# Moving one constant's load ahead of a weight tile, and a step's weight products ahead of its last attention blocks

## The chip, the cores and the metric

The kernel runs on one core of a Trainium2 chip. Time is device time in microseconds (us). The kernel before has a median of 446.83 us over 6 runs (446.69 to 450.45). The core's engines work side by side, each on its own list of instructions in order: TensorE (PE, with its weight loads PEld), VectorE (DVE), ScalarE (ACT), GpSimd (POOL) and SyncE (SP). Here POOL mostly issues transfers.

## The reference, cut to what matters

Two operators follow each other. The first is causal attention with a forget gate, for 8 batches, 8 heads, 576 positions and head size 64:

```python
scores = scale * q @ k.T                       # (8, 8, 576, 576)
decay  = cum[:, :, :, None] - cum[:, :, None, :]    # cum = cumsum(log(f))
attn   = softmax(where(causal, -1e9, scores + decay))
x      = (attn @ v), heads side by side        # (8, 576, 512)
```

The second mixes x along the sequence in the frequency domain, with one complex 512 x 512 matrix for each of 64 kept modes, and then mixes channels:

```python
X  = rfft(x, axis=1)[:, :64]
Yr = einsum("bmd,mde->bme", Xr, w_r) - einsum("bmd,mde->bme", Xi, w_i)
Yi = einsum("bmd,mde->bme", Xr, w_i) + einsum("bmd,mde->bme", Xi, w_r)
u  = x + irfft(Y, n=576)
out = u + relu(u @ w_ch)
```

`w_r` and `w_i` are 64 x 512 x 512 float32 each, 134 MB together. `w_ch` is 512 x 512 float32. Every weight of `w_r` and `w_i` is used once for each batch.

## The kernel before, in words

**Weights.** The two mode arrays are cut into 64 tiles of two transfers (`w_r`, `w_i`). Each transfer reads 1 MB of float32 and writes 512 KB of bf16, converted on the way. A tile is `emit_w_load(n)` (line 91), issued by POOL at line 89. The tiles live in a ring `wb` of 9 buffers (`NRING`, line 57), so the load of tile n may start only when the products with tile n - 9 are finished. The products are `emit_modes(n)` (line 118): 32 small matmuls into one PSUM tile `A` (line 146; the pool `psM` has one buffer during the attention), then one DVE instruction that stores `A` or adds it into `Yacc` (lines 155 and 157). Tiles 0 to 31 use the channels 0 to 255 of x (`dc` 0 and 1), and tiles 32 to 63 the channels 256 to 511, so that these need the whole attention to be over.

**Attention.** There are 32 steps s: a pair of heads `dc`, a pair of batches `bp`, one head h of the two; two successive steps make a pair `pr`. The loop is at line 649. A step emits, in this order: (a) in an even step the loads of k, q and v for pair `pr + 2` (`emit_loads`, line 215, on POOL); (b) in steps 0 to 8 a further weight tile, up to tile 8, which fills the ring; (c) the transposes of the next pair (`tp`, line 453: k and q in an even step, v in an odd one); (d) the first piece of the step's scores (`ps`, line 505) with their exponential on ACT (`E`, line 512) and the mask on DVE (line 527); (e) the first three row blocks of the product of the previous step's weights with v (`emit_av(s - 1, [0, 1, 2])`: `pav`, line 550, 16 matmuls, then a reciprocal and a scaling on DVE, lines 561 and 572); (f) the second and third piece of the scores; (g) the last two row blocks, `emit_av(s - 1, [3, 4])`, 18 matmuls and two DVE instructions; (h) the fourth, small piece of the scores and `emit_vback(s)` (`vp` and `va`, lines 477 to 484); (i) in an even step the Fourier transform of the pair that is done (`emit_dft`: `px`, lines 593 and 618, into `XT`, line 629). From step 9 on, (j), a step ends with one or two calls of `emit_modes`, each followed by `next_w()` (line 640), the load of the next tile.

**After the attention** (line 756), the tiles 32 to 62 alternate with `emit_xw`, the product of x with `wch` (lines 718 and 729). The last tile and the outputs follow from line 901.

**Order.** POOL's transfers stay in program order (`pool_dma`, line 88), so one that waits holds back all behind it. On the other engines a planner at build time lists the instructions: what is emitted first comes first, but where an instruction isn't ready in the planner's model of the time, a later one that is ready goes ahead of it. So PE's order isn't the order of emission. Before the first k transposes of step 14 (119.55 us) the trace shows 13 blocks of 32 `A` matmuls on PE, while the loop has called `emit_modes` 6 times by the end of step 13. `XT` of `dc` 0, which all of the tiles 0 to 15 need, is complete after the transform that step 8 emits.

`wch` is loaded once, in step 10 (line 656): behind tile 9, which `next_w()` issues at the end of step 9, and behind the k, q and v of pair 7. Its first use is at line 729, at 278.83 us.

Of the kernel before, what the change touches and what calls it, by code (L numbers as in the profile page):

```python
# [15 lines left out]
def _strided(ap: bass.AP, free_dims, offset_elems: int = 0) -> bass.AP:  # L16
    new_ap = [list(ap.ap[0])] + [list(x) for x in free_dims]
    return bass.AP(tensor=ap.tensor, offset=ap.offset + offset_elems, ap=new_ap)
# [3 lines left out]
def kernel(  # L22
# [12 lines left out]
    B, H, S, Dh = q.shape  # L35
# [43 lines left out]
    NTH = NT // 2  # L79
# [3 lines left out]
    def tile_of(n):  # L83
        if n < NTH:
            return divmod(n, NG)
        return 2, (n - NTH + GL) % NTH

    def pool_dma(dst, src):
        tc.keep_in_program_order(nc.gpsimd.dma_start(dst, src))  # L89

    def emit_w_load(n):
        dc, g = tile_of(n)
        if n < NTH:
            wb = wpool.tile([128, MG, 2 * D], BF16, tag="wb", name="wb")
            for t, src in enumerate((moe_w_r, moe_w_i)):
                pool_dma(
                    wb[t:128:2, :, :],
                    src[
                        g * MG : (g + 1) * MG, dc * 128 : (dc + 1) * 128, :
                    ].rearrange("m (p r) e -> p m (r e)", r=2),  # L100
                )
        else:
            wb = wpool.tile([128, 2, M2, 2 * D], BF16, tag="wb", name="wb")
            parts = 2 if n == NT - 1 else 1
            for h in range(parts):
                ms = slice(h * M2 // parts, (h + 1) * M2 // parts)
                for t, src in enumerate((moe_w_r, moe_w_i)):
                    pool_dma(
                        wb[:, t, ms, :],
                        src[g * M2 : (g + 1) * M2, D // 2 : D, :][ms].rearrange(  # L110
                            "m (p r) e -> p m (r e)", r=2
                        ),
                    )
        wtiles[n] = wb
# [3 lines left out]
    def emit_modes(n):  # L118
        dc, g = tile_of(n)
        wb = wtiles.pop(n)  # L120
        nm = MG if n < NTH else M2
        if late["psM"] is None:
            z = late["psZ"].tile([128, 2, D], F32, tag="z", name="A")
            A = z[:, 0, 0 : NDC * nm * 2 * B].rearrange(
                "p (e m c) -> p e m c", e=NDC, m=nm
            )
        else:
            A = late["psM"].tile([128, NDC, nm, 2 * B], F32, tag="A", name="A")
        if n < NTH:
            terms = [  # L130
                (lambda mi, es, r=r: wb[:, mi, r * D + es : r * D + es + 128],
                 lambda m, r=r: XT3s[dc][:, r, :, m])
                for r in (0, 1)
            ]
        else:
            terms = [
                (lambda mi, es, t=t, r=r: wb[:, t, mi, r * D + es : r * D + es + 128],
                 lambda m, c0=c0, r=r: XT3s[2 + r][:, m, c0 : c0 + 2 * B])
                for t, c0 in ((0, B), (1, 0))
                for r in (0, 1)  # L140
            ]
        for mi in range(nm):
            m = g * nm + mi
            for eb in range(NDC):
                for i, (w_of, x_of) in enumerate(terms):
                    nc.tensor.matmul(  # L146
                        A[:, eb, mi, :],
                        lhsT=w_of(mi, eb * 128),
                        rhs=x_of(m),
                        start=(i == 0),  # L150
                        stop=(i == len(terms) - 1),
                    )
        ysl = Yacc[:, :, g * nm : (g + 1) * nm, :]
        if n < NG:
            nc.vector.tensor_copy(ysl, A[:, :, :, :])
        elif n < NTH:
            nc.vector.tensor_tensor(ysl, A[:, :, :, :], ysl, ALU.add)
        else:
            n8 = nm * 2
            yt, w = (late["YTl"], GL * n8) if g < GL else (late["YT"], 2 * NM)  # L160
            nc.vector.tensor_tensor(  # L161
                _strided(
                    yt[:, 0, 0, g * n8 : g * n8 + 1], [[B * w, NDC], [w, B], [1, n8]]
                ),
                _strided(A[:, 0, 0, 0:1], [[nm * 2 * B, NDC], [1, B], [B, n8]]),
                _strided(
                    Yacc[:, 0, g * nm, 0:1], [[NM * 2 * B, NDC], [1, B], [B, n8]]
                ),
                ALU.add,
            )  # L170

    with ExitStack() as actx:
# [42 lines left out]
        def emit_loads(pr):  # L215
            dc, bp, _ = steps[2 * pr]
            for nm, src in (("k", k), ("q", q), ("v", v)):
                one = src[2 * bp, 2 * dc, :, :]
                dst = QKVst[pr % STG][nm][:, :, :, :].rearrange("p b r d -> p b (r d)")
                ap = bass.AP(  # L220
                    tensor=one.tensor,
                    offset=one.offset,
                    ap=[[NR * Dh, 128], [H * S * Dh, 2], [1, NR * Dh]],
                )
                if nm == "v" and pr < 2:
                    nc.sync.dma_start(dst, ap)
                else:
                    pool_dma(dst, ap)
# [268 lines left out]
        def emit_scores(s, piece):  # L497
            E = Es[s % NE]
            w = sum(x[2] for x in PIECES[piece])
            ps = psS.tile([128, 2, 512], F32, tag="sc", name="ps")  # L500
            h, pr = s % 2, s // 2
            for jb, c0, n, o in PIECES[piece]:
                for b in range(2):
                    bs = slice(b * 64, b * 64 + 64)
                    nc.tensor.matmul(  # L505
                        ps[:, b, o : o + n],
                        lhsT=KTs[pr % 2][bs, h, jb * 128 : (jb + 1) * 128],
                        rhs=QT[pr][bs, h, jb * 128 + c0 : jb * 128 + c0 + n],
                        start=True,
                        stop=True,  # L510
                    )
            nc.scalar.activation(  # L512
                E[:, :, piece * 512 : piece * 512 + w],
                ps[:, :, 0:w],
                ACT.Exp,
                scale=scale,
            )
            tri = trimask[:, :]
            if piece == 2:
                dg = _strided(E[:, 0, EOFF[2] : EOFF[2] + 1], [[EW, 2], [320, 2], [1, 128]])  # L520
                tr = _strided(tri, [[0, 2], [0, 2], [1, 128]])
            else:
                jb = {0: 0, 1: 1, 3: 4}[piece]
                n = 64 if piece == 3 else 128
                dg = E[:, :, EOFF[jb] : EOFF[jb] + n]
                tr = _strided(tri, [[0, 2], [1, n]])
            nc.vector.tensor_tensor(dg, dg, tr, ALU.mult)  # L527
# [108 lines left out]
        NS = len(steps)  # L636
        nload = 2
        nmode = 0

        def next_w():  # L640
            nonlocal nload
            if nload < NDC * NG:
                emit_w_load(nload)
                nload += 1
# [4 lines left out]
        for s in range(NS + 1):  # L649
            pr, h = s // 2, s % 2  # L650
            if h == 0 and pr + STG - 1 < NPR:
                emit_loads(pr + STG - 1)
            if s < 10 and nload < min(NRING, 3 + 3 * s // 4):
                next_w()
            if s == 10:
                pool_dma(wch[:], moe_w_ch.rearrange("(eb p) e -> p eb e", p=128))
            if pr + 1 < NPR:
                emit_transposes(pr + 1, ("kq", "v")[h])
            if s < NS:
                emit_scores(s, 0)  # L660
            if s >= 1:
                emit_av(s - 1, [0, 1, 2])
            if s < NS:
                emit_scores(s, 1)
                emit_scores(s, 2)
            if s >= 1:
                emit_av(s - 1, [3, 4])
            if s < NS:
                emit_scores(s, 3)
                emit_vback(s)  # L670
            if s >= 1:
                vaugs.pop(s - 1)
                if h == 0:
                    emit_dft(pr - 1)
            if s > B:
                while nmode < (s - B) * NTH // (NS - B):
                    emit_modes(nmode)
                    nmode += 1
                    next_w()

    with ExitStack() as bctx:
        bsb = bctx.enter_context(tc.tile_pool(name="bsb", bufs=1))
# [255 lines left out]
```

The softmax here doesn't subtract the row's maximum and nothing guards it: scores larger than these inputs give would overflow.

## Time and profile before

| what | value |
|---|---|
| median of 6 runs | 446.83 us |
| profiled execution, its own time | 446.75 us |
| its span, first to last instruction | 445.0 us |
| PE busy | 337.1 us (76%), mean granted clock 0.796 |
| DVE busy | 240.5 us (54%) |
| ACT busy | 197.8 us (44%) |
| POOL's transfers (queue 0) | 85.34 MB, 98.3% of 16 engines over the span |
| read from HBM / written to it | 163.73 MB / 9.44 MB |

Busy times are sums of the instructions' durations. A share of the 16 transfer engines is the time that all packets took over 16 times the stretch, and packets overlap, so a full queue shows 1.1 to 1.2 and not 1.0. GB/s count the bytes written. "Landing" is the time from the issue of a transfer by POOL until its last part has arrived. `[17.32 <-PE A L146]` after an instruction says that its engine stood idle for 17.32 us before it, and what ended the wait.

### The profile page before, as it was taken

The numbers are of one execution on the slowest core, as the hardware profiler recorded it, in microseconds if no ns is written. First come the engines' busy times: TensorE is split into PE (matmuls) and PEld (weight loads), VectorE is DVE, ScalarE is ACT, GpSimd is POOL, SyncE is SP. The second block draws the span as 40 slices with busy tenths as digits, with TensorE's granted clock in tenths as the row PEclk, the third lists the DMA queues.
The fourth block names the chain that finished last, engine by engine and source line by source line (L and its number), as shares of the span: only waits on it lengthen the run. The fifth ranks groups of instructions, "written<-read, shape, count | busy, mean of one in ns | idle before, by whom it ended". The sixth has DMA issues, their size and how long they took to land.

```text
span 445.0 us, 11215 instructions
## 1 busy us (share of the span) xinstructions
PE 337.1 (76%) x4823; PEld 232.7 (52%) x4823; DVE 240.5 (54%) x614; ACT 197.8 (44%) x296; POOL 138.4 (31%) x194
## 2 busy tenths in 40 slices
PE   2388888999797887977878896999982247527993
PEld 1256556687665566656655675566662124323441
DVE  5768988878466564655566675233230002103993
ACT  3378877776344636336536381334420002102442
POOL 7333330532332323323323221132343232200661
PEclk9999999999665857558668596899995558856998
DMA  8999999699999999999999999999999999991697
GB/s 203 211 235 238 237 237 236 116 236 212 236 237 210 237 217 230 237 217 230 237 217 231 211 212 211 211 209 211 211 212 210 211 211 211 211 195 31 224 378 278
DMA packets 50048, 97.27 MB, mean 219 GB/s; under 512 B 3376, under 2 KB 12080, under 8 KB 50000
## 3 DMA queue, kind: packets, MB, share of 16 engines
q0 software_dynamic: 46096, 85.34, 98.3%
q1 hardware_dynamic: 3824, 11.09, 6.9%
q8 instruction: 38, 0.62, 0.5%
q10 hardware_dynamic: 80, 0.13, 0.1%
q14 instruction: 10, 0.08, 0.0%
HBM read 163.73 MB, written 9.44 MB: 389 GB/s over the span
## 4 chain that ended last, share of the span: by engine, by line
PE 45%; DMA 20%; ACT 14%; DVE 10%; issue 4%; POOL 0%; DVEq 0%; ACTq 0%
DMA wb<-in_moe_w_i_dram 16%; ACT E L512 10%; PE pxw L729 7%; PE A L146 7%; PE pav L550 7%; PE ps L505 6%; PE tp L453 5%; DMA stv<-in_v_dram 3%; DVE QTs L468 2%; ACT KT L466 2%; PE ptr L718 2%; PE vp L477 2%; PE px L593 2%; PE pz L832 1%; DVE E L527 1%
## 5 line engine op out<-in xcount | busy, mean ns | idle before, releaser
L512 ACT ACTIVATE E<-ps 128x1024 bf16<-128x1024 f32 (+1 forms) x128 | 101.4, 853 | 21.3 <-PE ps L505 14.9
L146 PE MATMUL A<-XT,wb 128*128 128x16 bf16 x2048 | 71.7, 182 | 44.9 <-DMA wb<-in_moe_w_i_dram 24.0
L146 PEld LDWEIGHTS <-wb 128*128 128x128 bf16 x2048 | 64.7, 101 | 56.0 <-DMA wb<-in_moe_w_i_dram 25.9
L89 POOL DMA_DIRECT2D wb<-in_moe_w_r_dram x65 | 43.6, 671 | 153.4 <-PE A L146 52.5
L505 PE MATMUL ps<-QTs,KT 64*128 64x64 bf16 (+4 forms) x384 | 57.0, 316 | 17.6 <-ACT E L512 16.9
L89 POOL DMA_DIRECT2D wb<-in_moe_w_i_dram x65 | 43.4, 667 | 63.8 <-DMA wb<-in_moe_w_r_dram 31.6
L550 PE MATMUL pav<-va,E 128*128 128x65 bf16 (+1 forms) x1088 | 54.5, 209 | 2.8 <-DVE va L483 1.5
L550 PEld LDWEIGHTS <-E 128*128 128x128 bf16 (+1 forms) x1088 | 45.1, 114 | 16.0 <-issue 8.8
L527 DVE TENSOR_TENSOR E<-E,trimask 128x256 bf16<-128x256 bf16 (+2 forms) x128 | 37.0, 303 | 20.3 <-ACT E L512 20.0
L161 DVE TENSOR_TENSOR YT<-A,Yacc 128x128 bf16<-128x128 f32 x24 | 8.8, 369 | 68.1 <-PE A L146 68.1
L470 ACT COPY VT<-tp 128x640 bf16<-128x640 bf16 (+1 forms) x32 | 23.3, 760 | 31.4 <-PE tp L453 31.3
L505 PEld LDWEIGHTS <-KT 64*128 64x128 bf16 x384 | 19.0, 98 | 30.4 <-issue 21.6
L729 PE MATMUL pxw<-wch,yy 128*128 128x512 bf16 x144 | 34.2, 388 | 0.0
L736 ACT CAST XW<-pxw 128x512 bf16<-128x512 f32 x36 | 20.3, 587 | 30.6 <-PE pxw L729 25.1
L466 ACT COPY KT<-tp 128x640 bf16<-128x640 bf16 (+1 forms) x32 | 21.9, 744 | 26.8 <-PE tp L453 26.8
L468 DVE COPY QTs<-tp 128x640 bf16<-128x640 bf16 (+1 forms) x32 | 23.2, 767 | 13.6 <-PE tp L453 13.4
L572 DVE TENSOR_TENSOR x_all<-pav,rcp 128x384 bf16<-128x384 f32 x64 | 29.1, 455 | 0.8
L748 ACT CAST yy<-pyw 128x512 bf16<-128x512 f32 x8 | 4.7, 585 | 51.5 <-PE pyw L741 51.5
L877 POOL TENSOR_TENSOR uo<-uo 128x1024 f32<-128x1024 f32 x7 | 16.5, 2359 | 29.3 <-DVE uo L870 25.6
L441 DVE TENSOR_TENSOR vb<-stv,wdec 128x1152 bf16<-128x1152 f32 x16 | 21.6, 1352 | 3.5 <-PE tp L453 3.4
L561 DVE RECIPROCAL rcp<-pav 128x6 f32<-128x6 f32 x64 | 12.1, 190 | 20.7 <-PE pav L550 20.1
L729 PEld LDWEIGHTS <-yy 128*128 128x128 bf16 x144 | 13.6, 100 | 17.2 <-DVE yy L723 4.5
(115 smaller groups left out, 461.7 us busy)
## 6 DMA issues: line engine op xcount, KB each, us to landing
wb<-in_moe_w_r_dram POOLq DMA_DIRECT2D x63, 512.0 KB, 16.3
wb<-in_moe_w_i_dram POOLq DMA_DIRECT2D x63, 512.0 KB, 16.6
out_dram<-uo SPq DMA_DIRECT2D x16, 512.0 KB, 3.8
stv<-in_v_dram POOLq DMA_DIRECT2D x14, 576.0 KB, 15.1
stk<-in_k_dram POOLq DMA_DIRECT2D x16, 288.0 KB, 15.2
stq<-in_q_dram POOLq DMA_DIRECT2D x16, 288.0 KB, 15.2
stv<-in_v_dram SPq DMA_DIRECT2D x2, 576.0 KB, 6.4
out_dram<-uo SPq DMA_DIRECT2D x7, 128.0 KB, 4.3
```

The source lines that it names most:

```text
L89: tc.keep_in_program_order(nc.gpsimd.dma_start(dst, src))
L146: nc.tensor.matmul(A[:, eb, mi, :], lhsT=w_of(mi, eb * 128), rhs=x_of(m), start=(i == 0), stop=(i == len(terms) - 1),)
L453: nc.tensor.transpose(tp[:, r - r0, :, :].rearrange("c h p -> c (h p)"), sb[:, r, :, :].rearrange("p b d -> p (b d)"), ident_bf[:, :],)
L466: nc.scalar.copy(rows(KTs[pr % 2][:, :, 0:S]), tv)
L468: nc.vector.tensor_copy(rows(QT[pr][:, :, :]), tv)
L470: nc.scalar.copy(rows(VTs[pr % 2][:, :, 0:S]), tv)
L505: nc.tensor.matmul(ps[:, b, o : o + n], lhsT=KTs[pr % 2][bs, h, jb * 128 : (jb + 1) * 128], rhs=QT[pr][bs, h, jb * 128 + c0 : jb * 128 + c ...
L512: nc.scalar.activation(E[:, :, piece * 512 : piece * 512 + w], ps[:, :, 0:w], ACT.Exp, scale=scale,)
L527: nc.vector.tensor_tensor(dg, dg, tr, ALU.mult)
L550: nc.tensor.matmul(pav[64 * half : 64 * half + w, slot, :], lhsT=E[:, b, c : c + (w - 1) * st + 1 : st], rhs=va[:, jb, b, :], start=(n == ...
L572: nc.vector.tensor_tensor(xo, pi, ri, ALU.mult)
L729: nc.tensor.matmul(pxw[:, :], lhsT=xT[:, eb, i * 128 : (i + 1) * 128], rhs=wch[:, eb, :], start=(eb == 0), stop=(eb == NDC - 1),)
```

## The change

The load of `wch` is emitted one step earlier, at the start of step 9. On POOL's queue it so stands ahead of the two transfers of tile 9, and ahead of the k, q and v of pair 7. The block that calls `emit_modes` and `next_w` moves within each step: it stood at the end, and now stands between the third piece of the scores and `emit_av(s - 1, [3, 4])`. No instruction is added or removed.

```diff
-            if s == 10:
+            if s == 9:
                 pool_dma(wch[:], moe_w_ch.rearrange("(eb p) e -> p eb e", p=128))
...
             if s < NS:
                 emit_scores(s, 1)
                 emit_scores(s, 2)
+            if s > B:
+                while nmode < (s - B) * NTH // (NS - B):
+                    emit_modes(nmode)
+                    nmode += 1
+                    next_w()
             if s >= 1:
                 emit_av(s - 1, [3, 4])
             if s < NS:
...
                 if h == 0:
                     emit_dft(pr - 1)
-            if s > B:
-                while nmode < (s - B) * NTH // (NS - B):
-                    emit_modes(nmode)
-                    nmode += 1
-                    next_w()
```

## The prediction

> **What bounds the kernel now.** I read the page first, then the chain that ended last, then short stretches of time.
>
> ```profile
> DMA  8999999699999999999999999999999999991697
> GB/s 203 211 235 238 237 237 236 116 236 212 236 237 210 237 217 230 237 217 230 237 217 231 211 212 211 211 209 211 211 212 210 211 211 211 211 195 31 224 378 278
> ```
>
> The transfer engines are full in all of the 40 slices but the eighth (78 to 89 us), until the last weights are in at about 403 us. No other engine is full for as long. The chain ends accordingly: weight transfers one behind the other, then a tail.
>
> ```profile
> 328.00 1.42 POOL wb L89 x2
> 329.42 18.91 DMA wb<-in_moe_w_i_dram
> 348.62 19.74 DMA wb<-in_moe_w_i_dram
> 368.65 19.67 DMA wb<-in_moe_w_i_dram
> 388.61 14.67 DMA wb<-in_moe_w_i_dram
> ```
>
> So the end is set by when the stream of transfers ends; the 41.7 us from 403.3 to 445.0 (last products, outputs) follow it and are not touched. What counts is holes in the stream. Stretches of 1 us show the only one:
>
> ```profile
> 77.00:78.00 1.00, 1.00 (x10) 0.58 (x7) 0.86 (x3) 0.17 (x2) 0.00 (x0) 1.00 1.15 217
> 78.00:79.00 1.00, 1.00 (x22) 0.74 (x22) 0.69 (x1) 0.50 (x1) 0.00 (x0) 1.00 0.61 113
> 79.00:80.00 1.00, 1.00 (x22) 0.77 (x21) 0.54 (x2) 1.00 (x2) 0.00 (x0) 1.00 0.23 41
> 80.00:81.00 1.00, 1.00 (x34) 1.00 (x32) 0.70 (x2) 0.94 (x3) 0.00 (x0) 1.00 0.06 16
> 81.00:82.00 1.00, 1.00 (x23) 0.67 (x20) 0.82 (x4) 0.31 (x1) 0.43 (x1) 1.00 0.00 0
> 82.00:83.00 1.00, 1.00 (x19) 0.74 (x19) 0.98 (x5) 0.98 (x2) 1.00 (x3) 1.00 0.02 8
> 83.00:84.00 1.00, 1.00 (x24) 0.63 (x23) 1.00 (x4) 1.00 (x2) 1.00 (x2) 1.00 0.80 111
> ```
>
> (The last two columns are the share and GB/s.) POOL's list gives the cause: the ring is full, and tile 9 waits 17.32 us for the first products.
>
> ```profile
> 63.64 0.62 POOL L89 DMA_DIRECT2D wb<-in_moe_w_i_dram  x1 [1.77 <-DMA wb<-in_moe_w_r_dram]
> 81.57 0.81 POOL L89 DMA_DIRECT2D wb<-in_moe_w_r_dram  x1 [17.32 <-PE A L146]
> ...
> 85.10 0.80 POOL L89 DMA_DIRECT2D wch<-in_moe_w_ch_dram  x1
> 86.40 0.62 POOL L89 DMA_DIRECT2D wb<-in_moe_w_r_dram  x1 [0.51 <-PE A L146]
> ```
>
> **The hole's size.** The last transfer ahead of it (issued 63.64) takes 16.6 us to land: 80.2. The next (issued 81.57) takes 5.3 us, with nothing ahead of it: 86.9. In the full stream a 512 KB transfer follows the other by 524,288 B / 211 GB/s = 2.5 us. The hole is 86.9 - 80.2 - 2.5 = 4.2 us.
>
> **Part 1, `wch` into the hole.** It is one transfer of 512 KB. It lands 11.9 us after 85.10, at 97.0; v ahead of it lands at 84.38 + 10.2 = 94.6. So it takes 2.4 us of the full stream. Now it comes ahead of tile 9, on a POOL that stands idle from 64.3 to 81.6 us; its own issue (0.80 us) lies in that idle time, and its buffer has no earlier user. It can be issued when one more old transfer has landed, at about 66 us, and lands at 80.2 + 2.5 = 82.7 instead of idle time. Behind tile 9 the stream is then 2.4 us shorter. It passes five transfers (two of tile 9, three of k, q, v); the wait of tile 9 doesn't depend on it. Gain 2.4 us; bounds: nothing if the stream never notices, 4.2 us, the whole hole.
>
> **Part 2, the products earlier in the step.** A call issues 32 matmuls (1.17 us at 80.10), one DVE instruction (0.42 us at 81.31) and two POOL issues (0.8 and 0.6 us). Among POOL's transfers the move changes no order, and SP has none. On PE it passes 18 `pav` matmuls (0.70 us at 78.58), two `ps` (0.2 us) and five `vp` (0.45 us), in even steps the transform too; on DVE it passes a reciprocal, a scaling (0.18 and 0.36 us) and the `va` copies (0.49 us).
>
> For tile 9 only the first call counts:
>
> ```profile
> 78.22 0.69 DVE L629 CAST XT<-px 128x512 bf16<-128x512 f32 x1 [0.29 <-PE px L618]
> ```
>
> ```profile
> 78.40 0.25 PE L505 MATMUL ps<-QTs,KT 64*128 64x192 bf16 x1
> 78.58 0.70 PE L550 MATMUL pav<-va,E 128*128 128x65 bf16 x18
> ...
> 79.81 0.45 PE L477 MATMUL vp<-ident_bf,VT 128*128 128x128 bf16 x5
> 80.10 1.17 PE L146 MATMUL A<-XT,wb 128*128 128x16 bf16 x32
> ```
>
> `XT` is ready at 78.91, and the products start at 80.10. They can come earlier by at most 1.2 us. At the least they come no earlier, when the planner leaves them behind `vp`; a loss would need something new ahead of them, and the move puts nothing there. If they go right behind the 18 `pav` matmuls, which fill the wait for `XT`, it is 80.10 - 79.3 = 0.8 us: that is the value I take. If the planner puts them ahead of `pav`, PE stands for about 0.4 us, with `pav`, `ps` and `vp` behind it; PE's 1 us is not the stream's.
>
> In the later steps I cost the move at nothing. PE already runs products ahead of their emission (13 done by 119.55 us, 6 emitted), so they are gap fillers whatever their place in a step, and POOL waits for earlier transfers (29.4 and 25.8 us of waits between 119 and 276 us), not for PE (4.1 us). That cover is gone after 262 us, see next.
>
> Sum in the hole: 2.4 + 0.8 = 3.2 of 4.2 us; tile 9 would still land 1.0 us late.
>
> **What is late next.** Behind the attention the ring is empty again: tile 41 waits for the first products that need the whole of x.
>
> ```profile
> 277.20 0.71 POOL L89 DMA_DIRECT2D wb<-in_moe_w_r_dram  x1 [8.52 <-PE A L146]
> ...
> 297.04 0.71 POOL L89 DMA_DIRECT2D wb<-in_moe_w_r_dram  x1 [4.91 <-PE A L146]
> ```
>
> The answer for the transfers issued from 296.5 to 298.3 us ends:
>
> ```profile
> DMA to landing us min/median/max: 8.2/9.1/10.0
> ```
>
> Alone such a transfer took 5.3 us, so 8.2 - 5.3 = 2.9 us of older work were left in the queue at 297 us: the smallest cover after the first hole (9.6 at 290.69 gives 4.3). PE is full from 280 to 330 us (10.00 of 10 us in each stretch) and sets these issues. A stream that is 3.2 us early meets a PE that is not: it runs dry for 0.3 us. Sum: 3.2 - 0.3 = 2.9 us, if the attention ends when it did. From 446.75 us of the profiled execution (span 445.0 and 1.75 around it) this is 443.85; the median, 446.83, is 0.08 above that execution: forecast 443.9 us. (About 0.5%, 2.2 us, is what a measurement can tell from no change here.)
>
> **Two rules of the Trainium skill.** The row: a lone 512 KB transfer landed 5.3 us after its issue. "DMA: Bandwidth & Descriptors", section "Anatomy of one DMA — SWDGE (gpsimd) path", fits one as 2.0 us plus bytes over 436 GB/s, by my estimate 3.2 us. By the row the refill stays 1.0 us late; by the page it would be in time and the hole would close, 4.2 us. The row is this kernel's, with float32 read and converted, so I stay with it. The second row: from 116 to 120 us PE was granted a clock of 0.50 with no wait longer than 0.6 us. [...]
>
> **Rivals.**
>
> 1. *The gain is eaten at 297 us.* The attention ends 0.7 to 5 us later, or cover is lost otherwise; each us later than now costs one us. For: the cover there is 2.9 us and PE is full. Against: tiles 10 to 12 and k, q, v come earlier, and all 31 early products are done at 261 us. Time 444.6 to 449.0.
> 2. *The attention ends earlier and the hole closes.* Products fill PE's waits for ACT, 11.4 us of `ps` waits between 119 and 276 us. Then no 0.3 us are lost and up to 4.2 us are gained: 442.6.
> 3. *Slower: the attention's pace.* The pairs of steps between 119.55 and 247.18 us (starts of the k transposes) take 17.2 to 19.5 us. Products ahead of the last blocks delay `pav`, so the exponential that reuses `E`, and PE waits at half clock. If the four fast pairs (17.2 to 17.9) became slow ones (19.3), the attention would end some 7.5 us later, at 284 instead of 276 us. Then 7.5 - 2.9 = 4.6 us are lost: 451.4. It decides from 2.9 us of delay on, and shows beyond 5.1 us.
> 4. *The planner's list hardly changes and `wch` alone counts:* 2.4 us, all within the cover of 2.9, so 444.4. It lies in the forecast's own range.
>
> **How the numbers follow.** Chances: forecast with rival 4 (443.2 to 444.6) 0.52; rival 2 (below 443.2) 0.06; rival 1 0.22; rival 3 0.20, because the planner's order can't be read from this trace. Faster 0.58, no difference 0.22, slower 0.20. The range starts at rival 2's 442.6 and goes up until no more than 0.1 lies above it, half of rival 3: 449.5. The forecast's own range is 443.2 to 444.6.
>
> **What would show it.** Right: `wch` issued near 66 us and landing near 83; tile 9 issued at 80.3 to 81; the share of the transfer engines not at 0 in any 1 us before 400; the last `w_i` landing near 400.4 instead of 403.3. Wrong: a second hole between 285 and 300 us, or tile 41 issued later than 280 us. The prediction fails if the order on PE after 120 us changes so much that the first products of tile 32 come more than 0.7 us later.

## The result, and the profile after

The changed kernel takes 444.77 us (median of 21 runs, 443.74 to 446.70), the kernel before 447.82 us (median of 47, 446.49 to 452.91). The ratio is 0.9932, with a 95% interval of 0.9919 to 0.9945: 3.0 us faster (2.5 to 3.6). The profiled execution of after took 446.11 us with a span of 444.1 us. It is among the longer ones of after, as the one of before (446.75 us) is among the shorter ones of before, so these two profiles alone show a difference of 0.6 us. Further profiles of the same code, below, are needed to see the whole.

First the page of after, share of the transfer engines and GB/s in 40 slices:

```profile
DMA  8999999999999999999999999999999999991697
GB/s 205 210 236 237 236 237 237 165 236 215 232 237 212 236 236 212 236 234 213 236 231 218 210 211 211 197 193 201 211 211 212 210 212 210 212 206 25 225 379 278
```

The eighth slice has risen from 116 to 165 GB/s. But slices 26 to 28 (278 to 311 us; the count begins at 0, the eighth slice is number 7), which had 209 to 211 before, have fallen to 193 to 201: a second hole that the kernel before didn't have. POOL's list of after shows the first hole's cause half gone:

```profile
63.58 0.61 POOL L89 DMA_DIRECT2D wb<-in_moe_w_i_dram  x1 [1.78 <-DMA wb<-in_moe_w_r_dram]
66.04 0.74 POOL L89 DMA_DIRECT2D wch<-in_moe_w_ch_dram  x1 [1.85 <-DMA wb<-in_moe_w_i_dram]
81.85 0.61 POOL L89 DMA_DIRECT2D wb<-in_moe_w_r_dram  x1 [15.07 <-PE ps L505]
```

`wch` is issued at 66.04, as soon as one older transfer has landed. Tile 9 still waits for PE. (The releaser's name is the PE instruction that happened to come last; the products start at 80.39.) The lists of transfers in two short windows of after (66 to 67 us and 81 to 83.1 us) give the landings in the last column:

```profile
wch<-in_moe_w_ch_dram POOLq DMA_DIRECT2D x1, 512.0 KB, 16.9
```

```profile
wb<-in_moe_w_r_dram POOLq DMA_DIRECT2D x1, 512.0 KB, 5.0
```

`wch` lands at 66.04 + 16.9 = 82.9 and tile 9's first half at 81.85 + 5.0 = 86.9. With 2.5 us for a transfer in the full stream, 86.9 - 82.9 - 2.5 = 1.5 us of the 4.2 us are left. The stretches of 1 us of after agree (last two columns: share, GB/s):

```profile
80.00:81.00 1.00, 1.00 (x29) 0.95 (x26) 0.84 (x3) 1.00 (x3) 0.00 (x0) 1.00 1.00 165
81.00:82.00 1.00, 1.00 (x24) 0.81 (x20) 0.84 (x3) 0.88 (x2) 0.15 (x1) 1.00 0.61 103
82.00:83.00 1.00, 1.00 (x13) 0.49 (x11) 0.98 (x4) 0.50 (x1) 1.00 (x2) 1.00 0.07 11
83.00:84.00 1.00, 1.00 (x26) 0.92 (x25) 0.43 (x3) 1.00 (x2) 1.00 (x3) 1.00 0.82 98
```

On PE, the first products stand where the working put them, behind the 18 `pav` matmuls and ahead of `vp` (PE's timeline of after):

```profile
79.39 0.70 PE L550 MATMUL pav<-va,E 128*128 128x65 bf16 x18
80.02 0.20 PE L505 MATMUL ps<-QTs,KT 64*128 64x64 bf16 x1
80.15 0.40 PE L453 MATMUL tp<-ident_bf,vb 128*128 128x128 bf16 x4
80.39 1.17 PE L146 MATMUL A<-XT,wb 128*128 128x16 bf16 x32
81.49 0.20 PE L505 MATMUL ps<-QTs,KT 64*128 64x64 bf16 x1
81.62 0.45 PE L477 MATMUL vp<-ident_bf,VT 128*128 128x128 bf16 x5
```

From the start of `pav` to that of the products it is 1.00 us, where it was 1.52: 0.5 us earlier in their step. That step itself began 0.8 us later in this execution (`pav` at 79.39 against 78.58). PE is at its own pace there, and that pace differs from one execution to the next: tile 9 was issued at 81.57 and 82.19 us in two profiles that have before's order on PE up to there, and at 81.39 to 81.85 us in three of the changed kernel (table below).

Behind the attention, POOL's list and stretches of 2 us of after show the second hole:

```profile
278.47 0.71 POOL L89 DMA_DIRECT2D wb<-in_moe_w_r_dram  x1 [12.35 <-PE A L146]
...
285.85 0.71 POOL L89 DMA_DIRECT2D wb<-in_moe_w_r_dram  x1 [5.95 <-PE ptr L718]
...
291.18 0.71 POOL L89 DMA_DIRECT2D wb<-in_moe_w_r_dram  x1 [3.90 <-PE ptr L718]
```

```profile
284.00:286.00 2.00, 2.00 (x44) 1.62 (x43) 0.42 (x2) 1.17 (x2) 0.15 (x1) 1.00 1.12 211
286.00:288.00 2.00, 2.00 (x17) 0.99 (x14) 1.28 (x4) 0.04 (x1) 1.28 (x2) 1.00 0.86 143
...
292.00:294.00 2.00, 2.00 (x11) 0.83 (x10) 0.89 (x3) 0.56 (x2) 0.61 (x1) 1.00 1.14 173
...
298.00:300.00 2.00, 2.00 (x22) 1.24 (x20) 1.70 (x5) 0.00 (x0) 2.00 (x4) 1.00 1.08 175
```

POOL waited 12.35 us for the first products of tile 32 (8.52 before): the stream was ahead, PE was not. In this execution PE was also late: tile 41 was issued at 278.47 us, 1.27 us later than in the profile of before. In two further profiles of the changed kernel it was issued at 276.87 and 277.58 us, and the hole was there too. The transfers issued at 285.85, 291.18 and 297.51 landed after 6.8, 7.0 and 7.2 us, where a transfer with nothing ahead of it took 5.0. The chain of after ends as before, with weight transfers and a tail:

```profile
347.49 19.60 DMA wb<-in_moe_w_i_dram
367.38 19.60 DMA wb<-in_moe_w_i_dram
387.26 14.60 DMA wb<-in_moe_w_i_dram
```

The last weights are in at 401.9 us instead of 403.3, and the tail takes 42.2 us (41.7 before).

### The profile page after: what moved, and what is told of

It reads as the page before. It is cut to its first block, busy times and chain, and to the rows that moved or that the text cites. A ratio compares the mean times of both kernels' runs of the same rounds, so it can differ in the third digit from the quotient of the medians.

```text
span 444.1 us, 11213 instructions
## 1 busy us (share of the span) xinstructions
PE 339.7 (77%) x4823; PEld 233.5 (53%) x4823; DVE 241.5 (54%) x614; ACT 198.3 (45%) x296; POOL 138.3 (31%) x194
## 4 chain that ended last, share of the span: by engine, by line
PE 48%; DMA 16%; ACT 14%; DVE 10%; issue 4%; POOL 0%; DVEq 0%; ACTq 0%
DMA wb<-in_moe_w_i_dram 16%; ACT E L512 10%; PE pav L550 8%; PE A L146 7%; PE pxw L729 7%; PE ps L505 7%; PE tp L453 6%; DVE QTs L468 3%; PE vp L477 2%; PE px L593 2%; ACT KT L466 2%; PE ptr L718 2%; PE pz L832 2%; DVE E L527 1%; DVE XT L607 1%
## 5 line engine op out<-in xcount | busy, mean ns | idle before, releaser
L505 PE MATMUL ps<-QTs,KT 64*128 64x64 bf16 (+4 forms) x384 | 58.7, 326 | 17.5 <-ACT E L512 17.1
```

The source lines that it names most:

```text
L505: nc.tensor.matmul(ps[:, b, o : o + n], lhsT=KTs[pr % 2][bs, h, jb * 128 : (jb + 1) * 128], rhs=QT[pr][bs, h, jb * 128 + c0 : jb * 128 + c ...
```

## The experiments

Two things were in doubt. Is the stream of transfers the cause, or the new order on PE? And what took back part of the gain? All ratios are against the kernel before on the same chip, with 95% intervals; where a gain in us differs a little from the difference of the two medians, it is the ratio's; "the late start" is the condition on `emit_xw` that the third experiment adds.

### One part alone: only the load of wch

```diff
-            if s == 10:
+            if s == 9:
                 pool_dma(wch[:], moe_w_ch.rearrange("(eb p) e -> p eb e", p=128))
```

> Only the load of wch is moved, the products stay at the end of each step. Hole theory (the stream of transfers sets the end, and wch fills 2.4 of the 4.2 us in which it stands still): 2.4 us faster than before, ratio 0.9946; wch is issued near 66 us, and tile 9 near 81.6 us as before. Order theory (the gain comes from the new order on PE and not from the hole): no difference, ratio 1.000 within 0.001, because the orders on PE differ little from before.

Measured: 445.28 us against 448.33, ratio 0.9930 (0.9903 to 0.9957), 3.1 us. The hole theory's 0.9946 lies inside, the order theory's 1.000 outside. `wch` was issued at 66.46 us and tile 9 at 82.00; the hole is as in after, a little wider:

```profile
80.00:81.00 1.00, 1.00 (x25) 0.86 (x23) 0.59 (x2) 1.00 (x2) 0.00 (x0) 1.00 1.09 181
81.00:82.00 1.00, 1.00 (x27) 0.72 (x24) 0.82 (x3) 0.38 (x2) 0.00 (x0) 1.00 0.55 93
82.00:83.00 1.00, 1.00 (x22) 0.69 (x21) 1.00 (x5) 0.87 (x1) 1.00 (x2) 1.00 0.09 14
83.00:84.00 1.00, 1.00 (x16) 0.68 (x15) 0.99 (x6) 0.98 (x2) 1.00 (x2) 1.00 0.57 45
```

This part alone gives what the whole change gives, within the intervals.

### The other part alone: only the products

The same diff as the change's second part, with `wch` left in step 10.

> Only the products are moved ahead of the last two AV blocks; wch stays in step 10. Hole theory: tile 9 is issued 0.5 to 0.8 us earlier relative to its step and nothing else counts, 0.5 to 0.8 us faster than before, ratio 0.998 to 0.999. Order theory: nearly the whole gain of the change, ratio 0.994. If the products put off the attention's end (first products of tile 32 finished later than 277.2 us), the cover of 2.9 us at 297 us hides it and the time stays.

Measured: 446.93 us against 448.33, ratio 0.9963 (0.9936 to 0.9989), 0.5 to 2.9 us. Tile 9 was issued at 81.35 us, and the hole remained (shares 0.30, 0.03, 0.07 and 0.28 from 79 to 83 us). The expected 0.5 to 0.8 us lie in the interval, the order theory's ratio of 0.994 as well. The profile accounts for about 0.5 us: the first hole is 4.1 us instead of 4.6 (table below). The time alone can't separate the two; the last experiment bears on it.

### The second hole: later products of x with wch

Tile 41 is issued when the products of tile 32 are done, and then a block of `emit_xw` stands behind the products of each of the tiles 32, 33 and 34 (in after's list of PE 6.8, 4.7 and 5.7 us from the first transpose to the end). Here they start after tile 36, so that five buffers come free at once:

```diff
-                if nmode % 4 and nx < B:
+                if nmode > NTH + 4 and nmode % 4 and nx < B:
                     emit_xw(nx)
```

On the changed kernel:

> The changed kernel, and behind the attention the products of x with wch start only after the products of tiles 32 to 36, so that five ring buffers come free at once. Theory that a second hole (286 to 302 us, where the changed kernel's stream fell from 211 to about 190 GB/s) takes back what the first hole gave: it closes, and the kernel is 1 to 2 us faster than the changed one, ratio to before 0.989 to 0.991. Rival, that the stream is not what ends last any more (the attention's end or PE's own work sets it): no gain over the changed kernel, ratio 0.993.

On the kernel before:

> The kernel before with the same late start of the products of x with wch. Theory: before, the stream never runs dry behind the attention (2.9 us of older work were left at 297 us), so nothing is to be had there: ratio 1.000 within 0.001. Rival, that the late start helps by itself (less work on PE between the tiles, another order): the same gain as in the changed kernel, ratio 0.995 to 0.998.

Measured: on the changed kernel 444.62 us, ratio 0.9910 (0.9880 to 0.9939), an interval with both the theory's 0.991 and the rival's 0.993 in it; on the kernel before 447.78 us, ratio 0.9982 (0.9955 to 1.0009), no difference that can be told, though the rival's 0.998 isn't excluded by the time. To compare with the changed kernel on one chip, both were run once more:

> The changed kernel as the reference for the next three, on one chip with them: ratio to before 0.993.

> The changed kernel with the late start of the products of x with wch, beside the changed kernel on one chip. If the second hole takes back part of the gain: 0.5 to 2 us faster than the changed kernel. If it doesn't: the same within 0.3 us.

Measured: 445.56 us for the changed kernel (444.39 to 447.34, 9 runs; ratio 0.9935, 0.9910 to 0.9961) and 444.31 us with the late start (443.68 to 445.12, 6 runs; 0.9908, 0.9877 to 0.9939): 1.25 us between the medians. The intervals overlap, but the profile is plain on the second hole. (The 1.25 us are not the second hole's alone: tile 9 was issued at 81.01 us in the one profile and at 81.47 in the other, with the same order on PE, and the first hole was 0.9 us instead of 1.7.) POOL's list and the same stretches as above, of the changed kernel with the late start:

```profile
276.47 0.71 POOL L89 DMA_DIRECT2D wb<-in_moe_w_r_dram  x1 [10.57 <-PE A L146]
277.18 0.72 POOL L89 DMA_DIRECT2D wb<-in_moe_w_i_dram  x1
277.89 0.73 POOL L89 DMA_DIRECT2D wb<-in_moe_w_r_dram  x1
278.60 0.74 POOL L89 DMA_DIRECT2D wb<-in_moe_w_i_dram  x1
279.31 0.75 POOL L89 DMA_DIRECT2D wb<-in_moe_w_r_dram  x1
```

```profile
284.00:286.00 2.00, 2.00 (x14) 0.94 (x13) 0.00 (x0) 1.37 (x3) 0.72 (x1) 1.00 1.12 211
286.00:288.00 2.00, 2.00 (x51) 1.71 (x50) 1.11 (x4) 0.59 (x1) 0.29 (x1) 1.00 1.12 211
292.00:294.00 2.00, 2.00 (x32) 1.45 (x29) 1.78 (x5) 0.01 (x1) 0.71 (x1) 1.00 1.13 212
298.00:300.00 2.00, 2.00 (x68) 2.00 (x65) 1.02 (x4) 0.35 (x1) 0.54 (x1) 1.00 1.12 211
```

The stream stays at 211 GB/s throughout: the second hole is gone. In the kernel before there was none to close: with the late start its last weights came in at 403.9 us, without it at 403.3.

### Only wch, with the late start

> Only wch is moved, the products of a step stay at its end, and the products of x with wch start after those of tile 36, so that the second hole is closed. Theory that the two parts of the change add up where no second hole caps them (wch 2.4 us, earlier products 0.5 to 1.3 us): 2.4 to 3.0 us faster than before, ratio 0.9935 to 0.9945, which is 0.5 to 1.3 us slower than the changed kernel with the same late start (0.991). Rival, that the earlier products gave nothing beyond wch: 0.991, the same as that kernel.

Measured: 445.40 us against 447.70, 2.3 us between the medians; the ratio, 0.9939 (0.9915 to 0.9963, so 2.7 us), is inside the range of the first theory. The stream has no second hole, and 2.2 us of the first are left (table below). Its rival, 0.991, lies just outside the interval.

### Something else into the hole

Here `wch` and the products stay as before, and the k, q and v of pair 7 go ahead of tile 9:

```diff
-            if h == 0 and pr + STG - 1 < NPR:
+            if h == 0 and s != 10 and pr + STG - 1 < NPR:
                 emit_loads(pr + STG - 1)
+            if s == 9:
+                emit_loads(7)
```

> The kernel before, with only the loads of k, q and v of pair 7 moved from step 10 to step 9, ahead of tile 9; wch and the products stay. Theory that any transfer that is needed anyway fills the hole: 4.2 us of stream lie in a hole of 4.2 us; the second place has 2.9 us of cover, so 2.9 to 3.3 us faster than before, ratio 0.9925 to 0.9935. Rival, that wch matters for itself (its place behind k, q and v delayed something): no difference, 1.000.

Measured: 445.03 us (443.58 to 448.48, 12 runs), ratio 0.9945 (0.9921 to 0.9968), 2.5 us. The expected 0.9925 to 0.9935 lie in the interval, the rival (1.000) does not: `wch` isn't the only transfer that can fill the hole. In its profile the first hole is nearly gone, but the second is the widest of all. Stretches of 2 us:

```profile
286.00:288.00 2.00, 1.83 (x35) 1.47 (x33) 1.56 (x5) 0.31 (x1) 1.29 (x2) 1.00 0.75 141
288.00:290.00 2.00, 2.00 (x11) 0.94 (x10) 0.13 (x1) 1.07 (x2) 0.14 (x1) 1.00 1.00 162
...
294.00:296.00 2.00, 2.00 (x11) 0.88 (x9) 0.00 (x0) 1.49 (x3) 0.00 (x0) 1.00 0.84 129
```

There is a third low place, which no other kernel here has to this extent. Tile 11 was issued at 94.32 us, after a wait of 6.21 us for the products that free its buffer. Two stretches of 1 us behind it:

```profile
97.00:98.00 1.00, 1.00 (x13) 0.55 (x11) 1.00 (x2) 1.00 (x2) 1.00 (x3) 1.00 0.82 115
98.00:99.00 1.00, 1.00 (x27) 0.80 (x25) 1.00 (x3) 1.00 (x2) 1.00 (x2) 1.00 0.92 152
```

The profiled execution took 447.69 us, 2.7 us above the median of its 12 runs, so what its holes cost is not what they cost in a usual run.

### Both holes closed

The changed kernel, with the late start, and with k, q and v of pair 7 loaded in step 9 behind `wch`:

```diff
             if s == 9:
                 pool_dma(wch[:], moe_w_ch.rearrange("(eb p) e -> p eb e", p=128))
+                emit_loads(7)
```

The changed kernel as its reference, and then this version:

> The changed kernel once more, on the chip of the next three, as their reference: ratio to before 0.993, and the stream at about 190 to 205 GB/s in part of the time from 286 to 302 us, in a profile whose tile 9 was issued early in relation to before.

> The changed kernel with both holes closed: k, q and v of pair 7 (4.2 us of stream) are loaded at the start of step 9 too, ahead of tile 9, and the products of x with wch start after those of tile 36. Hole theory: the first hole is gone (share of the transfer engines above 1.0 in each 1 us from 77 to 88 us), and so is the second: 4.2 to 4.8 us faster than before, ratio 0.989 to 0.9905. Rival, that the second hole alone was left and the first is already filled: as the changed kernel with the late start alone, 0.991. Rival, that something else sets the end by now (PE, or the tail): 0.993.

Measured on that chip: the changed kernel 444.81 us (0.9925, 0.9898 to 0.9952), this version 444.08 us (0.9908, 0.9875 to 0.9942). Once more on the chip of the third reference run:

> Both holes closed (wch and k, q, v of pair 7 ahead of tile 9, late start), beside the changed kernel on one chip: 0.5 to 2 us faster than the changed kernel, and 0 to 1 us faster than the one with the late start alone, since 1 us or less of the first hole was left.

Measured: 444.06 us (443.05 to 444.84), ratio 0.9899 (0.9868 to 0.9930), 1.5 us below the changed kernel there and 0.25 us below the late start alone. Of the two ratios the first, 0.9908, is just outside the expected 0.989 to 0.9905, the second inside. The rival of 0.991, the late start alone, lies in both intervals, so the times don't show that closing the rest of the first hole gave more; the profile shows that it is closed. Stretches of 1 us:

```profile
81.00:82.00 1.00, 1.00 (x13) 0.63 (x12) 0.98 (x4) 0.42 (x2) 0.78 (x2) 1.00 1.22 207
82.00:83.00 1.00, 1.00 (x24) 0.72 (x22) 0.47 (x3) 1.00 (x2) 0.53 (x1) 1.00 1.19 204
```

### Both holes closed, products at the end of the step

The version above, without the change's second part.

> Both holes closed in the same way, but the products of a step stay at its end as before. Theory that the earlier products are worth only the earlier issue of tile 9: with the hole full of other transfers that issue is in time anyway (82 us plus 5.3 us of landing, against about 89 us when the stream gets there), so the time is that of the version with earlier products, within 0.4 us. Rival, that the earlier products help the attention by themselves: 0.5 to 1.5 us slower than that version.

Measured: 444.07 us (443.05 to 446.27), ratio 0.9902 (0.9868 to 0.9937), the same as the version with earlier products (444.06). So where another transfer fills the hole, the place of the products in the step is worth nothing that can be told; the runs spread from 443.05 to 446.27 us, so some tenths either way can't be excluded. The last weights came in at 398.7 us, against 399.5 and 398.8 with the earlier products. That speaks for tile 9's earlier issue, and not a faster attention, as the source of what this part gave alone.

### What the profiles say together

The first hole is taken here as the sum over the stretches of 1 us from 77 to 88 us of what the share lacks to 1.12, divided by 1.12. The last column is the issue of the last transfer plus its landing.

| kernel | tile 9 issued | first hole | tile 41 issued | 2nd hole seen | last weights in |
|---|---|---|---|---|---|
| before | 81.57 | 4.6 | 277.20 | no | 403.3 |
| before, late start | 82.19 | 5.0 | 277.50 | no | 403.9 |
| only products | 81.35 | 4.1 | 276.89 | no | 402.8 |
| only wch | 82.00 | 2.1 | 276.74 | yes | 401.3 |
| only wch, late start | 81.83 | 2.2 | 275.87 | no | 401.3 |
| only k, q, v | 82.05 | 0.8 | 278.29 | yes | 403.1 |
| change (three profiles) | 81.85, 81.39, 81.47 | 1.9, 1.4, 1.7 | 278.47, 276.87, 277.58 | yes | 401.9, 401.2, 401.4 |
| change, late start (two) | 80.80, 81.01 | 0.9, 0.9 | 274.72, 276.47 | no | 399.6, 400.3 |
| both closed (two) | 81.24, 81.22 | 0.1, 0.1 | 275.94, 277.31 | no | 399.5, 398.8 |
| both closed, products at the end | 81.36 | 0.1 | 274.08 | no | 398.7 |

Where there is no second hole, the last weights are in at 398.8 us plus the first hole, within 0.7 us: in these kernels the stream sets the end. What is above that in the others is put down here to the second hole: 401.9 - 398.8 - 1.9 = 1.2 us, and 1.0 and 0.9 us, in the three profiles of the change; 0.4 us with `wch` alone, which is within the 0.7; 3.5 us with k, q and v alone, where tile 41 was among the latest and where the low place at 97 us is in the sum too.

The bytes give the price without this sum. Adding up the GB/s of the stretches of 1 us tells when each kernel had written as much as the kernel before; how much earlier is called its lead here (good to about 0.2 us). In the three profiles of the change the lead was 2.7, 3.0 and 2.8 us where before stood at 284 us, and 0.5, 1.4 and 1.5 us at 310 us: the second hole took 2.2, 1.6 and 1.3 us. With `wch` alone it took 0.9 us (2.3 to 1.4). With k, q and v alone the lead was already down to 2.5 us at 120 us, although the first hole was 3.8 us smaller, and the second hole then took 2.8 us. By the last landing a part of the change's loss is made up: its stream ends in a shorter time, with 137, 78 and 14 GB/s in the stretches of 1 us from 399 to 402 us, where that of before ends with 123, 102, 94 and 49 from 399 to 403 us.

## Why the prediction was right, point by point

- **What bounds the kernel.** Right. Every kernel's end follows the last landing by 41.6 to 42.7 us, and the last landing follows the holes.
- **The gain.** 2.9 us were forecast; the ratio gives 3.0 (2.5 to 3.6). The absolute time, 444.77 us, is 0.9 above the forecast 443.9, because the median of before was 446.83 over the six runs shown and is 447.82 over 47.
- **Part 1, 2.4 us.** Right: `wch` alone took the first hole from 4.6 and 5.0 us (two profiles with before's first hole) to 2.1 and 2.2 us, so by 2.4 to 2.9 us. Issued "near 66 us" and landing "near 83": 66.04 and 82.9.
- **Part 2, 0.8 us by the earlier first products.** Right in place (behind `pav`, ahead of `vp`). In its step the products came 0.5 us earlier instead of 0.8, since the four remaining `tp` matmuls stayed ahead; the first hole shrank by 0.2 to 1.3 us from `wch` alone (2.1 and 2.2) to the five profiles with both parts (1.9 to 0.9).
- **Later steps at nothing.** The conclusion held: 444.07 against 444.06 us. The cover was the one named: products as gap fillers. That PE's order would hardly change (rival 4) was so for the larger part. PE's timelines of the two profiles were compared, with neighbouring matmuls on one tile as one group: 22 of before's 83 groups between 80 and 120 us have no counterpart in after; from 120 to 280 us it is 3 of 174, and two executions of the changed kernel differ in 3 there as well. So behind 120 us there was next to nothing that could have cost or given time.
- **What is late next.** Right in place, wrong in size. The sum took off 0.3 us; the change's profiles show 0.9 to 1.2 us by the last landings and 1.3 to 2.2 us by the bytes. The step that failed is "8.2 - 5.3 = 2.9 us of older work", used as if the stream kept its rate until the queue is empty. In the change's first profile the stream was down to 143 to 175 GB/s at landings of 6.8 to 7.2 us, so with some 2 us of older work left; in the other two it fell to between 145 and 193 at landings of 6.7 to 8.4 us. Before, at 8.2 us, it was at 209 and then 201. So the landing doesn't tell the cover: about the same landing went with a full stream in one execution and with a hole in another. The first hole had shown that the rate falls early: from 78 to 81 us the share goes from 0.61 over 0.23 to 0.06, not at once. By lead less loss, the cover was 0.5, 1.4 and 1.5 us in the change's three profiles, not 2.9.
- **Why the sum still came out.** The medians' 3.0 us and the profiles don't fully agree: from before's profile to the three of the change the last landing moves by 1.4 to 2.1 us, from the profile of before with the late start (the same first hole, no second) by 2.0 to 2.7. With one or two profiles of each, and tile 9's issue moving by half a microsecond between executions, it can't be settled which execution is typical. So the agreement to 0.1 us is partly luck: the second hole alone was off by 0.6 to 1.9 us.
- **Rivals.** The first (the gain eaten at 297 us) is the one that came true in part, by the cover more than by a later attention: tile 41 was issued 1.3 us later than before in one profile of the change, but 0.3 us earlier and 0.4 us later in the other two. The second (hole closed, 442.6) needed further changes, and with them the best medians are 444.06 and 444.07 us. The third (attention slower by 7.5 us) did not: tile 41 was issued between 274.1 and 278.5 us in all 14 profiles, with no order by kernel, and twice the same code differs by up to 1.8 us.
- **The signs that were named.** `wch`'s issue and landing came as said, and in after's profile the share was above 0 in every 1 us from 3 to 400 us (0.07 at the least). Not as said: tile 9 was issued at 81.4 to 81.9 us instead of 80.3 to 81, and the last weights were in at 401.2 to 401.9 us instead of near 400.4. Of the signs of being wrong one came true, the second hole between 285 and 300 us; tile 41 was never issued later than 280 us.
- **The page on transfers.** For a lone transfer the row stood: 5.0 and 5.2 us in after and with `wch` alone, against the 3.2 us estimated from the Trainium skill's "DMA: Bandwidth & Descriptors", section "Anatomy of one DMA — SWDGE (gpsimd) path". At 3.2 us tile 9 would, by this estimate, have landed at 85.1 instead of 86.9, and no hole would have been left.
- **The clock in the attention.** No kernel changed the attention's pace, so no run tells what a further wait would cost. The profile of before shows that the granted clock can fall without a long wait: it went from 1.00 to 0.50 between 112 and 116 us, and the longest wait of PE from 84 to 116 us was 0.6 us.

## What to carry to other kernels

When a full stream of transfers sets the end, look for the stretches in which it runs dry, and put into them a transfer that is needed anyway and waits for nothing. Here `wch`, and k, q and v, each did it; the gain to expect is the transfer's own time in the stream, up to the size of the hole (2.4 us for `wch`, and its hole shrank by 2.4 to 2.9 us). Then look for the next place where the queue runs low, because the stream gets there earlier while the engine that frees the buffers does not: here 1 to 2 us were lost there, and the hole closed when several buffers were freed at once ahead of long work. The cheaper of two parts may do it all; here moving one line did, within the intervals, and with the hole full the other part was worth nothing that can be told.

## What the runs showed that had not been expected

- The stream loses rate well before its queue is empty: in the change's three profiles 143 to 193 GB/s instead of 211, in stretches in which a new transfer still took 6.7 to 8.4 us to land, against 5.0 to 5.2 with nothing ahead of it.
- Filling the first hole further than `wch` does, without freeing buffers earlier behind the attention, need not give more: the k, q and v alone left 0.8 us of the first hole and were not faster than `wch` alone (2.5 and 3.1 us by their ratios, intervals overlapping). In their profile, one of the longest of their runs, the lead was down to 2.5 us by 120 us, and the second hole took 2.8 us.
- The best version closes both holes and is 1.5 us below the changed kernel on the same chip, at 444.06 us, and needs no change in the place of the products.
